# Squared-ReLU attention with two feed-forward layers: kept blocks read by 512-byte pieces, queries permuted, rounding on ScalarE

## The chip, the cores and the metric

The kernel runs on one core of one Trainium2 chip. The metric is the device time of one execution in microseconds (us), the median of several runs. TensorE (PE) does the matmuls, VectorE (DVE) and ScalarE (ACT) the elementwise work, SyncE (SP) issues nearly all DMAs. Each engine takes its instructions in the order of the program.

## The reference

Attention without softmax, then a feed-forward layer with a shrunk tanh, then a channel mix; all in float32.

```python
def _attn_ref(u, v, z):                      # u, v: (4, 3072, 256), z: (4, 3072, 64)
    scores = (1.0 / S) * np.matmul(z, z.transpose(0, 2, 1))
    attn = np.maximum(scores, 0.0) ** 2
    return u * np.matmul(attn, v)

def _moe_ref(x, w_in, w_out):                # w_in: (256, 2048)
    h = x @ w_in
    return (h - np.tanh(h)) @ w_out

def _moe2_ref(x, mu_k, mu_r, w_k, w_v, w_r): # w_k: (256, 1024)
    x_prev = np.concatenate([np.zeros((B, 1, D)), x[:, :-1, :]], axis=1)
    xk = mu_k * x + (1.0 - mu_k) * x_prev
    xr = mu_r * x + (1.0 - mu_r) * x_prev
    k = np.maximum(xk @ w_k, 0.0)
    r = 1.0 / (1.0 + np.exp(-(xr @ w_r)))
    return r * (k * k @ w_v)
```

`scores` is symmetric in queries and keys, so `attn` is too.

## The kernel before

**Precision.** Each float32 operand of a matmul is split into a high part, rounded to the matmul's own format, and a low part, the rest. A product takes three matmuls (`PASSES`: high with high, high with low, low with high). `copy_hi` (L83) rounds on ScalarE, `sub_lo` (L86) takes the rest on VectorE. For the scores the low and high parts of z lie in the two halves of the partitions, so two matmuls do: `z1` against `z1`, and `z1` against `z2`, which is `z1` with its halves swapped. `z_swap` (L123) makes it by two DMAs from `z1`.

**Tiles and units.** The 12288 rows are 24 tiles `t` of 512, six (`g` = 0 to 5) in each of four batches. A tile's attention is 12 units of 256 keys each (a pair of key chunks `kp`). A computed ("fresh") unit is 4 score matmuls, then on ScalarE Relu (L318) and Square (L319), on VectorE the rounding (L320, a CAST) and the low part (L87), and 12 matmuls with v into the tile's accumulator. Its names are `w_A` (PSUM), `a_A`, `h_A`, `l_A`. A unit's 12 matmuls come two units later (`LAG`).

**Kept blocks.** `attn` being symmetric, a block of 512 by 512 that tile i computed for keys j is what tile j needs for keys i, transposed. Tiles i = 0, 1 and 2 (`AGAIN` = 3) store such blocks to HBM (`keep`, L345), and tiles j > i read them again. `again_load` (L349) brings a block in by 16 DMAs of 64 KB in pieces of 128 bytes (32 elements), so that 32x32 transposes on VectorE finish the transposition. A re-read unit is: transpose (L373), rounding on ScalarE (L84), low part on VectorE (L87); its names are `b`, `t`, `h_t`, `l_t`. Tile g reads min(g, 3) blocks, two units each. In tiles g = 3, 4 and 5 re-read and fresh units alternate, which makes six pairs a tile (`pairs`, L327). From one pair to the next the order of tile 2 is fresh, fresh, re-read.

**The order.** The program is written out in one order (L666 to 681). At each unit n: the loads due at n go to SyncE's queue (`loads`), then the store of the unit before, then `produce` for unit n, `consume` for unit n - 2, `turned_high` for unit n + 1 (transpose and rounding, if it is a re-read unit), and `run_steps`. That takes side steps from a list sorted by due time until a budget of VectorE time is spent (L645), and takes what is overdue in any case. The side steps of the attention are: z (transpose, round, low part) and v (ScalarE copy, VectorE low part) for the next batch, u's transpose (`u_turn`), the product with u (`x1_steps`), and, up to the fourth batch, the conversion of the weights from 64-bit floats (`c_steps`, four steps of two to three VectorE instructions, names `cw_` and `c_`). In the fourth batch's last units the weights are split (`w_steps`).

**Buffers that matter.** `scratch` (four tiles: `a_A` and `t`), `hi` and `lo` (three each), two PSUM tiles for scores. A scratch tile that a store reads is free when the store has landed.

After the attention come the feed-forward layers, tile by tile, units H, K and R, with `x2_steps` (L480), `mix_steps` and `out_steps`.

## Time and profile before

| | |
|---|---|
| time, median of 3 runs | 2685.3 us (2685.24 to 2689.43) |
| profiled execution, its own time | 2691.05 us |
| its span, first to last instruction | 2689.3 us |
| PE busy | 2626.3 us (98%), 11424 matmuls |
| VectorE busy | 1738.7 us (65%) |
| ScalarE busy | 1271.8 us (47%) |
| DMA | 719738 packets, 663920 of them under 512 bytes |

The attention fills the first 1049 us, the feed-forward layers the rest. A matmul's record is about 0.39 us long, but matmuls are pipelined and the next one starts earlier, so the share of PE busy says little; the count of matmuls in a stretch against its length says how near PE is to its pace. An engine's idle time stands in brackets behind the instruction that ended it, with what released it. SPq is SyncE's sequencer, which issues the DMAs.

### The profile page before, as it was taken

To read this page: it belongs to the slowest core of one execution; us is meant where nothing else is said; L and a number is where in the kernel's file an instruction comes from. 1 tells how busy PE (TensorE), PEld (TensorE's weight loads), DVE (VectorE), ACT (ScalarE), POOL (GpSimd) and SP (SyncE) were. 2 spreads that over 40 slices of the span, in tenths; PEclk is the share of its full clock that TensorE was granted. 3 is DMA by queue.
4 is the path that set the end of the run, shared out by engine and by line. 5 is a ranking of instruction groups with operands and counts; after the bars stand their busy time and mean duration, and the time that the engine had idled before them with its cause. 6 is when DMAs were issued, how large, how long until landed. Compare 5 with 4: busy or idle time off the path is not lost.

```text
span 2689.3 us, 29169 instructions
## 1 busy us (share of the span) xinstructions
PE 2626.3 (98%) x11424; PEld 2149.4 (80%) x11424; DVE 1738.7 (65%) x1876; ACT 1271.8 (47%) x1386; POOL 0.2 (0%) x4
## 2 busy tenths in 40 slices
PE   8989998999999999999999999999999999999998
PEld 7767776777778887888888888888888888888887
DVE  8788878977996777555555555555555555555554
ACT  6444544454455545444444444444444444444443
POOL 0000000000000000000000000000000000000000
PEclk9999999999999999999999999999999999999999
DMA  8788568857876772000000000000000000000000
GB/s 199 185 171 174 149 174 171 175 166 181 160 160 192 175 126 104 8 16 16 16 17 16 16 16 16 16 16 16 16 16 16 16 16 16 16 16 17 16 8 16
DMA packets 719738, 204.07 MB, mean 76 GB/s; under 512 B 663920, under 2 KB 676208, under 8 KB 719600
## 3 DMA queue, kind: packets, MB, share of 16 engines
q1 hardware_dynamic: 718544, 202.08, 32.4%
q8 instruction: 89, 1.46, 0.2%
q14 instruction: 49, 0.40, 0.0%
q10 hardware_dynamic: 1056, 0.13, 0.0%
HBM read 114.03 MB, written 82.05 MB: 73 GB/s over the span
## 4 chain that ended last, share of the span: by engine, by line
PE 70%; SPq 15%; DVE 6%; DMA 4%; issue 3%; ACT 2%; DVEq 0%; ACTq 0%
PE acc_H L464 19%; PE w_H L408 19%; PE acc_K L464 10%; PE w_K L408 10%; SPq L355 9%; PE acc_A L464 7%; SPq L158 3%; PE w_R L432 2%; DMA b<-at 2%; SPq L99 1%; DVE t L373 1%; PE w_A L396 1%; PE w_A L395 1%; DVE h_A L320 1%; DVE l_A L87 1%
## 5 line engine op out<-in xcount | busy, mean ns | idle before, releaser
L464 PE MATMUL acc_A<-h_A,v 128*128 128x512 f32 x1536 | 504.7, 391 | 1.4 <-DVE h_A L320 1.4
L464 PE MATMUL acc_H<-h_H,w_out 128*128 128x512 f32 x1536 | 504.0, 389 | 0.0
L408 PE MATMUL w_H<-xh,w_in 128*128 128x512 f32 x1536 | 500.4, 389 | 0.0
L84 ACT ACTIVATE h_H<-g_H 128x1024 fp32r<-128x1024 f32 x192 | 203.7, 1061 | 386.1 <-DVE g_H L422 386.1
L87 DVE TENSOR_TENSOR l_H<-g_H,h_H 128x1024 fp32r<-128x1024 f32 x192 | 235.3, 1226 | 216.3 <-ACT h_H L84 216.3
L422 DVE TENSOR_TENSOR g_H<-w_H,g_H 128x1024 f32<-128x1024 f32 x192 | 233.6, 1217 | 171.2 <-ACT g_H L421 171.2
L464 PEld LDWEIGHTS acc_A<-h_A,v 128*128 128x128 f32 x1536 | 289.0, 188 | 63.3 <-DVE h_A L320 3.7
L464 PEld LDWEIGHTS acc_H<-h_H,w_out 128*128 128x128 f32 x1536 | 288.3, 188 | 59.8
L408 PEld LDWEIGHTS w_H<-xh,w_in 128*128 128x128 f32 x1536 | 288.3, 188 | 59.8
L421 ACT ACTIVATE g_H<-w_H 128x1024 f32<-128x1024 f32 x192 | 195.7, 1020 | 243.9 <-PE w_H L408 243.6
L464 PE MATMUL acc_A<-l_A,v 128*128 128x512 f32 x768 | 302.3, 394 | 8.7 <-DVE l_A L87 7.9
L408 PE MATMUL w_H<-x,w_in 128*128 128x512 f32 x768 | 298.8, 389 | 0.0
L464 PE MATMUL acc_H<-l_H,w_out 128*128 128x512 f32 x768 | 298.8, 389 | 0.0
L84 ACT ACTIVATE h_t<-t 128x1024 fp32r<-128x1024 f32 x96 | 101.9, 1062 | 353.6 <-DVE t L373 353.6
L318 ACT ACTIVATE a_A<-w_A 128x1024 f32<-128x1024 f32 (+1 forms) x193 | 195.9, 1015 | 153.1 <-PE w_A L396 113.6
L464 PE MATMUL acc_A<-h_t,v 128*128 128x512 f32 x768 | 259.7, 401 | 0.0
L408 PE MATMUL w_K<-mkh,w_k 128*128 128x512 f32 x768 | 251.8, 389 | 0.0
L464 PE MATMUL acc_K<-h_K,w_v 128*128 128x512 f32 x768 | 251.8, 389 | 0.0
L87 DVE TENSOR_TENSOR l_A<-a_A,h_A 128x1024 fp32r<-128x1024 f32 (+1 forms) x193 | 235.5, 1220 | 6.6
L320 DVE CAST h_A<-a_A 128x1024 fp32r<-128x1024 f32 (+1 forms) x193 | 132.7, 688 | 116.2 <-ACT a_A L319 114.9
L319 ACT ACTIVATE a_A<-a_A 128x1024 f32<-128x1024 f32 (+1 forms) x193 | 203.9, 1057 | 6.1
L320 DVE CAST h_K<-a_K 128x1024 fp32r<-128x1024 f32 x96 | 66.7, 694 | 212.7 <-ACT a_K L319 212.7
(121 smaller groups left out, 3462.7 us busy)
## 6 DMA issues: line engine op xcount, KB each, us to landing
at<-a_A SPq DMA_DIRECT2D x96, 512.0 KB, 4.2
b<-at SPq DMA_DIRECT2D x768, 64.0 KB, 2.4
vr<-in_v_dram SPq DMA_DIRECT2D x24, 512.0 KB, 4.6
uin<-in_u_dram SPq DMA_DIRECT2D x192, 64.0 KB, 2.8
x1d<-x SPq DMA_DIRECT2D x24, 512.0 KB, 3.1
x<-x1d SPq DMA_DIRECT2D x24, 512.0 KB, 3.8
out_dram<-ot SPq DMA_DIRECT2D x192, 64.0 KB, 1.9
zin<-in_z_dram SPq DMA_DIRECT2D x94, 64.0 KB, 2.7
```

The lines of the kernel that those rows point to most:

```text
L84: nc.scalar.activation(out=o, in_=i, func=ACTF.Copy)
L87: nc.vector.tensor_tensor(out=o, in0=i, in1=hi.bitcast(F32), op=ALU.subtract)
L158: nc.sync.dma_start(out=a[32 * q : 32 * q + 32, c], in_=src[q])
L318: nc.scalar.activation(out=a[:, x], in_=w[:, x], func=ACTF.Relu, scale=sc)
L319: nc.scalar.activation(out=a[:, x], in_=a[:, x], func=ACTF.Square)
L320: nc.vector.tensor_copy(h[:, x], a[:, x])
L355: nc.sync.dma_start(out=t[32 * q : 32 * q + 32, c], in_=src[q, c])
L408: nc.tensor.matmul(w[:, j], ws[wt, f // 4][a][:, c, (f % 4) * P : (f % 4 + 1) * P], x[m][:, c], start=n == 0, stop=n == 3 * DC - 1,)
L421: nc.scalar.activation(out=g, in_=w, func=ACTF.Tanh)
L422: nc.vector.tensor_tensor(out=g, in0=w, in1=g, op=ALU.subtract)
L432: nc.tensor.matmul(w[:, d], ws["r", 0][a][:, c, d * P : (d + 1) * P], x[m][:, c], start=n == 0, stop=n == 3 * DC - 1,)
L464: nc.tensor.matmul(o[:, c], w[a][:, c * P : (c + 1) * P], s[m][:, j], start=p == 0 and j == 0 and n == 0, stop=p == last and j == 1 and n ...
```

## The change

- `again_load` reads a block by 4 DMAs of 256 KB, in pieces of 512 bytes (a whole 128-column row piece). Partition j of group q then holds rows m x 32 + j, m = 0 to 15, with 128 columns each.
- The transpose of a re-read unit is now two instructions, one for each key chunk, that pick their 32 columns out of each 128.
- Tiles 0 to 2, which keep blocks, work on permuted queries: column (a, b, i) of 4 x 4 x 32 stands at (b, a, i). For that there is `zq`, a permuted copy of `z1` on ScalarE, which is the moving operand of the scores, `z2` is made of it, u is transposed in two instructions into that order, re-read units of tiles 1 and 2 are written in it, and `x2_steps` puts the order back.
- In tiles g > 1 a fresh unit is rounded on ScalarE (`high=copy_hi`) and no longer on VectorE.
- The budget of side steps in tiles g > 1 is 2.1 at a fresh unit and 0.1 at a unit that is re-read (before 1.4 and 0.2), and what is left over, up to 1.0, or overspent is carried to the next unit, in the feed-forward layers too.

```diff
--- before.py
+++ after.py
@@ -41,6 +41,8 @@
 
 
 
+
+
     nc = tc.nc
     B, S, D = u.shape
     DQ = z.shape[2]
@@ -80,6 +82,13 @@
     zero = head[:, 4 * DC : 4 * DC + 1]
     x1d = [dr.tile([P, DC, TB], F32, name=f"x1d{t}") for t in range(NT)]
 
+    def swapped(x):
+
+        return x.rearrange("p (a b i) -> p b a i", a=4, b=4)
+
+    def columns(x):
+        return x.rearrange("p (a b i) -> p a b i", a=4, b=4)
+
     def copy_hi(o, i):
         nc.scalar.activation(out=o, in_=i, func=ACTF.Copy)
 
@@ -87,7 +96,7 @@
         nc.vector.tensor_tensor(out=o, in0=i, in1=hi.bitcast(F32), op=ALU.subtract)
 
 
-    zin, z1, z2, vraw, vs, uin, uT = {}, {}, {}, {}, {}, {}, {}
+    zin, z1, zq, z2, vraw, vs, uin, uT = {}, {}, {}, {}, {}, {}, {}, {}
 
     def z_load(b, g):
 
@@ -112,19 +121,24 @@
         def low():
             t, w = st["t"], st["w"]
             sub_lo(w[DQ:], t[DQ:], w[DQ:])
+            if g < AGAIN:
+                q = p2(f"zq_{b}_{g}", F32R)
+                copy_hi(columns(q), swapped(w.bitcast(F32)))
+            else:
+                q = w
             if b == 0 and g == 0:
                 z2[0] = w2 = p2("z2_0", F32R)
-                sub_lo(w2[:DQ], t[:DQ], w[:DQ])
-                copy_hi(w2[DQ:], t[DQ:])
-            z1[b, g] = w
+                sub_lo(columns(w2[:DQ]), swapped(t[:DQ]), swapped(w[:DQ]))
+                copy_hi(columns(w2[DQ:]), swapped(t[DQ:]))
+            z1[b, g], zq[b, g] = w, q
 
         return [(1.7, lambda: (high(), low()))]
 
     def z_swap(t):
         b, g = divmod(t, NG)
         w = p2(f"z2_{t}", F32R)
-        nc.sync.dma_start(out=w[:DQ].bitcast(F32), in_=z1[b, g][DQ:].bitcast(F32))
-        nc.sync.dma_start(out=w[DQ:].bitcast(F32), in_=z1[b, g][:DQ].bitcast(F32))
+        nc.sync.dma_start(out=w[:DQ].bitcast(F32), in_=zq[b, g][DQ:].bitcast(F32))
+        nc.sync.dma_start(out=w[DQ:].bitcast(F32), in_=zq[b, g][:DQ].bitcast(F32))
         z2[t] = w
 
     def v_load(b, g):
@@ -164,9 +178,16 @@
     def u_turn(t):
         a = uin.pop(t)
         w = p4(f"uT{t}")
-        nc.vector.transpose(
-            out=w.rearrange("p c t -> p (c t)"), in_=a.rearrange("p c k i -> p (c k i)")
-        )
+        if t % NG < AGAIN:
+            for c in range(DC):
+                nc.vector.transpose(
+                    out=w[:, c].rearrange("p (b a i) -> p b a i", a=4, b=4),
+                    in_=a[:, c].rearrange("p (a b) i -> p b a i", a=4),
+                )
+        else:
+            nc.vector.transpose(
+                out=w.rearrange("p c t -> p (c t)"), in_=a.rearrange("p c k i -> p (c k i)")
+            )
         uT[t] = w
 
 
@@ -310,14 +331,14 @@
     def scratch(name):
         return sb.tile([P, 2, 512], F32, tag="e", name=name, bufs=4)
 
-    def square_split(name, w, sc, pieces=1):
+    def square_split(name, w, sc, pieces=1, high=nc.vector.tensor_copy):
         a = scratch(f"a_{name}")
         h, l = parts(name)
         for j in range(pieces):
             x = slice(2 * j // pieces, 2 * (j + 1) // pieces)
             nc.scalar.activation(out=a[:, x], in_=w[:, x], func=ACTF.Relu, scale=sc)
             nc.scalar.activation(out=a[:, x], in_=a[:, x], func=ACTF.Square)
-            nc.vector.tensor_copy(h[:, x], a[:, x])
+            high(h[:, x], a[:, x])
             sub_lo(l[:, x], a[:, x], h[:, x])
         return a, h, l
 
@@ -348,11 +369,10 @@
 
     def again_load(b, g, i):
 
-        t = sb.tile([P, 4, 16, 32], F32, tag="big", name=f"b{b}_{g}_{i}", bufs=12)
-        src = kept[b, i, g].rearrange("(k j) (c a i) -> a c j k i", j=32, c=4, i=32)
-        for c in range(4):
-            for q in range(4):
-                nc.sync.dma_start(out=t[32 * q : 32 * q + 32, c], in_=src[q, c])
+        t = sb.tile([P, 16, 4 * 32], F32, tag="big", name=f"b{b}_{g}_{i}", bufs=12)
+        src = kept[b, i, g].rearrange("(m j) (q x) -> q j m x", j=32, q=4)
+        for q in range(4):
+            nc.sync.dma_start(out=t[32 * q : 32 * q + 32], in_=src[q])
         blocks[b, g, i] = t
 
     def is_again(n):
@@ -367,12 +387,18 @@
         t, q = divmod(n, NP)
         b, g = divmod(t, NG)
         kp = pairs[g][q]
-        x = blocks[b, g, kp // 2][:, kp % 2 * 2 : kp % 2 * 2 + 2]
+        x = blocks[b, g, kp // 2]
         a = scratch(f"t_{t}_{q}")
         h, l = parts(f"t_{t}_{q}")
-        nc.vector.transpose(
-            out=a.rearrange("p c t -> p (c t)"), in_=x.rearrange("p c k i -> p (c k i)")
-        )
+        for j in range(2):
+            f = kp % 2 * 2 + j
+            y = x[:, :, f * 32 : f * 32 + 32]
+            if g < AGAIN:
+                y = y.rearrange("p (c k) i -> p k c i", c=4)
+                o = a[:, j].rearrange("p (k c i) -> p k c i", k=4, c=4)
+            else:
+                o = a[:, j].rearrange("p (m i) -> p m i", i=32)
+            nc.vector.transpose(out=o, in_=y)
         copy_hi(h, a)
         turned[n] = (a, h, l)
 
@@ -392,9 +418,12 @@
             for j in range(2):
                 kc = 2 * kp + j
                 lhsT = z1[b, kc // 4][:, (kc % 4) * P : (kc % 4 + 1) * P]
-                nc.tensor.matmul(w[:, j], lhsT, z1[b, g], start=True, stop=False)
+                nc.tensor.matmul(w[:, j], lhsT, zq[b, g], start=True, stop=False)
                 nc.tensor.matmul(w[:, j], lhsT, z2[t], start=False, stop=True)
-            a, *split[unit] = square_split(name, w, scale, 2 if t == 0 and p == 0 else 1)
+            a, *split[unit] = square_split(
+                name, w, scale, 2 if t == 0 and p == 0 else 1,
+                copy_hi if g > 1 else nc.vector.tensor_copy,
+            )
             if (b, g, kp // 2) in kept:
                 stores[n + 1] = lambda: keep(b, g, kp, a)
         elif kind in ("H", "K"):
@@ -483,7 +512,10 @@
             x2t[i] = []
             for c in range(DC):
                 x = p2(f"x2_{i}_{c}")
-                nc.scalar.activation(out=x, in_=o[:, c], func=ACTF.Copy)
+                if i % NG < AGAIN:
+                    nc.scalar.activation(out=columns(x), in_=swapped(o[:, c]), func=ACTF.Copy)
+                else:
+                    nc.scalar.activation(out=x, in_=o[:, c], func=ACTF.Copy)
                 x2t[i].append(x)
 
         return [(0.2, f)]
@@ -633,7 +665,7 @@
         n = at["K", i, NK - 1] + LAG
         task(n, n + 2, out_steps, i)
     tasks.sort(key=lambda x: x[:3])
-    ready = []
+    ready, spare = [], [0.0]
 
     def run_steps(n):
 
@@ -642,7 +674,10 @@
             ready.append((x[0], list(x[3](*x[4]))))
         ready.sort(key=lambda x: x[0])
         kind = units[min(n, len(units) - 1)][0]
-        left = {"A": 0.2 if is_again(n) else 1.4, "H": 2.2, "K": 2.4, "R": 4.0}[kind]
+        left = {"A": 1.4, "H": 2.2, "K": 2.4, "R": 4.0}[kind]
+        if kind == "A" and n // NP % NG > 1:
+            left = 0.1 if is_again(n) else 2.1
+        left += spare[0]
         while ready and (left > 0 or ready[0][0] <= n):
             for x in list(ready):
                 if left > 0 or x[0] <= n:
@@ -651,6 +686,7 @@
                     left -= cost
                     if not x[1]:
                         ready.remove(x)
+        spare[0] = min(left, 1.0)
 
     with tc.manual_schedule():
         z_load(0, 0)
```

What this makes of the order is shown at three places. The first is ScalarE in the second batch's tile 3 (unit 9) to tile 4 (unit 1). `h_t_` and `a_A_` carry the unit's number in the tile. ScalarE's order before:

```order
L318 ACTIVATE a_A_9_3700<-w_A_9_3695 128x1024
L319 ACTIVATE a_A_9_3700<-a_A_9_3700 128x1024
L84 ACTIVATE h_t_10_3720<-t_10_3719 128x1024
L318 ACTIVATE a_A_11_3747<-w_A_11_3742 128x1024
L319 ACTIVATE a_A_11_3747<-a_A_11_3747 128x1024
L84 ACTIVATE h_t_0_3767<-t_0_3766 128x1024
L318 ACTIVATE a_A_1_3824<-w_A_1_3819 128x1024
L319 ACTIVATE a_A_1_3824<-a_A_1_3824 128x1024
L84 ACTIVATE h_t_2_3844<-t_2_3843 128x1024
```

Three operations repeat there, a Relu, a Square and a round of t. ScalarE's order over the same units after the change:

```order
L339 ACTIVATE a_A_9_3508<-w_A_9_3503 128x1024
L340 ACTIVATE a_A_9_3508<-a_A_9_3508 128x1024
L93 ACTIVATE h_A_9_3509<-a_A_9_3508 128x1024
L93 ACTIVATE h_t_10_3528<-t_10_3527 128x1024
L93 ACTIVATE zq_0_3538<-z_2_0_3534 128x512
L339 ACTIVATE a_A_11_3558<-w_A_11_3553 128x1024
L340 ACTIVATE a_A_11_3558<-a_A_11_3558 128x1024
L93 ACTIVATE h_A_11_3559<-a_A_11_3558 128x1024
L93 ACTIVATE h_t_0_3578<-t_0_3577 128x1024
L93 ACTIVATE zq_1_3592<-z_2_1_3588 128x512
L339 ACTIVATE a_A_1_3628<-w_A_1_3623 128x1024
L340 ACTIVATE a_A_1_3628<-a_A_1_3628 128x1024
```

Behind each Square stands one more operation (`h_A`), and a `zq` stands between a round of t and the next Relu.

The second is VectorE over the same units, where `zt_` and `z_` are z's side step, `cw_` the weights' conversion. VectorE's order before:

```order
L373 STREAM_TRANSPOSE t_10_3719<-b_3_2_3429 128x1024
L109 STREAM_TRANSPOSE zt_1_3724<-zin_1_3601 128x512
L110 CAST z_2_1_3725<-zt_1_3724 128x512
L87 TENSOR_TENSOR z_2_1_3725<-zt_1_3724,z_2_1_3725 64x512
L87 TENSOR_TENSOR l_t_10_3721<-t_10_3719,h_t_10_3720 128x1024
L320 CAST h_A_11_3748<-a_A_11_3747 128x1024
L87 TENSOR_TENSOR l_A_11_3749<-a_A_11_3747,h_A_11_3748 128x1024
L373 STREAM_TRANSPOSE t_0_3766<-b_4_0_3549 128x1024
L204 TENSOR_SCALAR cw_in_1_3771<-c_in_1_3655 128x512
L208 SCALAR_TENSOR_TENSOR cw_in_1_3771<-c_in_1_3655,cw_in_1_3771 128x512
L211 TENSOR_SCALAR cw_in_1_3771<-c_in_1_3655 128x512
L87 TENSOR_TENSOR l_t_0_3768<-t_0_3766,h_t_0_3767 128x1024
```

Side steps stand there wherever a unit's budget lets them. VectorE's order over the same units after the change:

```order
L96 TENSOR_TENSOR l_t_10_3529<-t_10_3527,h_t_10_3528 128x1024
L96 TENSOR_TENSOR l_A_11_3560<-a_A_11_3558,h_A_11_3559 128x1024
L401 STREAM_TRANSPOSE t_0_3577<-b_4_0_3383 128x512 x2
L225 TENSOR_SCALAR cw_in_1_3583<-c_in_1_3475 128x512
L229 SCALAR_TENSOR_TENSOR cw_in_1_3583<-c_in_1_3475,cw_in_1_3583 128x512
L232 TENSOR_SCALAR cw_in_1_3583<-c_in_1_3475 128x512
L118 STREAM_TRANSPOSE zt_1_3587<-zin_1_3421 128x512
L119 CAST z_2_1_3588<-zt_1_3587 128x512
L96 TENSOR_TENSOR z_2_1_3588<-zt_1_3587,z_2_1_3588 64x512
L96 TENSOR_TENSOR l_t_0_3579<-t_0_3577,h_t_0_3578 128x1024
L96 TENSOR_TENSOR l_A_1_3630<-a_A_1_3628,h_A_1_3629 128x1024
```

The CAST (L320) is gone from between the transposes and the low part of A, the transposes are two, and side steps (`cw_`, `zt`, `z_`) stand only between a transpose and the low part of t.

The third is SyncE's queue around the swap for tile 2 of the first batch (`z_2`), with the kept blocks `b_2_0` and `b_2_1` and the stores (`at_`). SyncE's order before:

```order
L355 DMA b_2_0_760<-at_0_2_89 32x16x32 x16
L183 DMA c_in_1_777<-in_moe_w_in_dram 128x1024
L347 DMA at_1_5_98<-a_A_6_739 128x2x512
L347 DMA at_1_5_98<-a_A_7_785 128x2x512
L126 DMA z_2_823<-z_0_2_194 64x512
L127 DMA z_2_823<-z_0_2_194 64x512
L240 DMA wd_in_706<-cw_in_1_868 128x512
L158 DMA uin_928<-in_u_dram 32x16x32 x8
L355 DMA b_2_1_937<-at_1_2_90 32x16x32 x16
```

The swap (L126, L127) stands behind two stores and ahead of the next kept block. SyncE's order at the same place after the change:

```order
L375 DMA b_2_0_757<-at_0_2_89 32x16x128 x4
L204 DMA c_in_1_762<-in_moe_w_in_dram 128x1024
L368 DMA at_1_5_98<-a_A_6_735 128x2x512
L368 DMA at_1_5_98<-a_A_7_770 128x2x512
L140 DMA z_2_809<-zq_2_202 64x512
L141 DMA z_2_809<-zq_2_202 64x512
L261 DMA wd_in_702<-cw_in_1_855 128x512
L172 DMA uin_915<-in_u_dram 32x16x32 x8
L375 DMA b_2_1_924<-at_1_2_90 32x16x128 x4
```

The order of the queue is the same; each group of kept-block issues has 4 in place of 16, and the swap reads `zq`.

## Rows read from the trace of the kernel before

**Rows 1.** Windows, tiles 0–2 and 3–5 of each batch: length, engines' busy (count), clock

```profile
0.00:144.30 144.30, 132.37 (x557) 105.85 (x557) 113.18 (x139) 77.87 (x78) 0.20 (x4) 0.99 0.77 191
144.30:270.10 125.80, 115.02 (x478) 91.36 (x477) 110.79 (x134) 54.77 (x55) 0.00 (x0) 0.96 0.82 171
270.10:413.60 143.50, 136.83 (x582) 109.10 (x580) 112.22 (x138) 74.21 (x73) 0.00 (x0) 0.99 0.62 163
413.60:537.40 123.80, 113.80 (x477) 90.08 (x476) 110.52 (x134) 54.47 (x55) 0.00 (x0) 0.97 0.83 172
537.40:681.70 144.30, 137.23 (x582) 109.96 (x580) 112.53 (x138) 74.40 (x73) 0.00 (x0) 0.98 0.67 177
681.70:799.50 117.80, 111.90 (x478) 88.20 (x477) 110.19 (x134) 54.38 (x55) 0.00 (x0) 1.00 0.82 163
799.50:931.50 132.00, 131.77 (x582) 108.77 (x581) 92.66 (x92) 78.72 (x78) 0.00 (x0) 1.00 0.68 179
931.50:1049.10 117.60, 115.25 (x502) 94.91 (x501) 87.14 (x81) 58.00 (x59) 0.00 (x0) 0.99 0.60 128
```

**Rows 2.** Waits: engine and line, waited for what: us in total, times, longest

```profile
ACT a_A L318 <- DMA at<-a_A: 30.2, 11, 7.2
...
PE w_A L396 <- DMA z<-z: 7.4, 3, 3.5
```

**Rows 3.** SyncE's issues (duration ns min/median/max) and two landings from the chain

```profile
L355 SPq DMA_DIRECT2D b<-at x768: 302/487/3113, 57.7 to 1007.9; - x192
...
L347 SPq DMA_DIRECT2D at<-a_A x96: 359/434/1211, 16.6 to 926.4; - x96
...
66.25 3.25 DMA at<-a_A
...
90.10 5.69 DMA z<-z
```

**Rows 4.** Timeline of ScalarE and VectorE, fourth batch: start us, us, instruction

```profile
954.28 1.06 ACT L84 ACTIVATE h_t<-t 128x1024 fp32r<-128x1024 f32 x1 [3.49 <-DVE t L373]
955.24 1.01 ACT L318 ACTIVATE a_A<-w_A 128x1024 f32<-128x1024 f32 x1
955.37 1.23 DVE L87 TENSOR_TENSOR l_t<-t,h_t 128x1024 fp32r<-128x1024 f32 x1 [1.19 <-ACT h_t L84]
956.28 1.06 ACT L319 ACTIVATE a_A<-a_A 128x1024 f32<-128x1024 f32 x1
957.38 0.70 DVE L320 CAST h_A<-a_A 128x1024 fp32r<-128x1024 f32 x1 [0.78 <-ACT a_A L319]
958.11 1.23 DVE L87 TENSOR_TENSOR l_A<-a_A,h_A 128x1024 fp32r<-128x1024 f32 x1
959.25 1.24 DVE L373 STREAM_TRANSPOSE t<-b 128x1024 f32<-128x1024 f32 x1
960.58 1.06 ACT L84 ACTIVATE h_t<-t 128x1024 fp32r<-128x1024 f32 x1 [3.24 <-DVE t L373]
```

**Rows 5.** Timeline of the first batch's side steps on ScalarE and VectorE

```profile
219.96 0.38 DVE L204 TENSOR_SCALAR cw_in<-c_in 128x512 int32<-128x512 int32 x1
...
221.32 1.22 DVE L87 TENSOR_TENSOR l_t<-t,h_t 128x1024 fp32r<-128x1024 f32 x1
...
242.24 0.71 DVE L109 STREAM_TRANSPOSE zt<-zin 128x512 f32<-128x512 f32 x1
...
243.44 0.69 DVE L87 TENSOR_TENSOR z<-zt,z 64x512 fp32r<-64x512 f32 x1
...
247.37 1.06 ACT L84 ACTIVATE h_t<-t 128x1024 fp32r<-128x1024 f32 x1 [4.30 <-DVE t L373]
...
248.33 1.05 ACT L84 ACTIVATE v<-vr 128x1024 fp32r<-128x1024 f32 x1
```

**Rows 6.** Timeline at the program's start

```profile
11.53 1.01 ACT L318 ACTIVATE a_A<-w_A 128x1024 f32<-128x1024 f32 x1
...
13.93 0.69 DVE L87 TENSOR_TENSOR z<-zt,z 64x512 fp32r<-64x512 f32 x1
```

## The prediction, made before the changed kernel ran

> **What bounds the kernel now.** I read the windows by batch first [rows 1]. In the fourth batch's tiles 0 to 2 the matmuls run without a gap: 582 in 132.0 us, 0.2267 us each. Every stretch can be held against that pace, and what is over is TensorE time lost. Tiles 3 to 5 of the four batches lose 125.8 - 478 x 0.2267 = 17.4, 15.7, 9.4 and 3.8 us, 46.3 in all. Tiles 0 to 2 lose 18.0, 11.6, 12.4 and 0.1, together 42.1. The feed-forward part behind them is hardly touched by the diff, so only these 88 us are in play. They have two sources.
>
> The first is SyncE's queue. The waits show ScalarE held 30.2 us by stores of kept blocks that had not landed (their scratch tile is to be used again), and TensorE 7.4 us by the z swap [rows 2]. Behind both stands the same thing: 768 issues of 64 KB at about 0.49 us, 16 in a row for each kept block [rows 3]. Sixteen take 16 x 0.53 = 8.5 us with the step between them, and a store or a swap behind them starts that much later. The rows of the chain show one store landing after 3.25 us and one swap after 5.69 [rows 3].
>
> The second is a ring of two in-order engines. In tiles 3 to 5 re-read and computed units alternate. ScalarE does: round t, Relu, Square; VectorE does: round A (CAST), A's low part, transpose of the next t, and that releases ScalarE's next round. From one round of t to the next it is 954.28 to 960.58, 6.30 us [rows 4]. TensorE needs 28 matmuls per pair, 28 x 0.2267 = 6.35. So the ring stands 0.05 us under TensorE's pace, and any step put on it is lost. The fourth batch, which has no side work until its last units, shows that it just holds.
>
> **Part 1, the loads.** 16 issues per block become 4, 768 become 192. Price of one issue: the 512 KB store takes 0.434 us, the 64 KB load 0.487 [rows 3], so bytes don't set it; 4 x 0.53 = 2.1 us stand where 8.5 stood, and a store or swap behind is 6.4 us earlier. That covers the stall of most of these waits. Of the 42.1 us of tiles 0 to 2 I keep 10 for the program's start (TensorE's first matmul can't run until z is there) and 6 for VectorE's side steps, and book 26 as gone. The bounds are 7.4 (the swaps alone [rows 2]) and 32 (all but the start). That the fourth batch loses 0.1 us with the same loads says that the queue hurts only together with the c, z and v loads, and these stay. In tiles 3 to 5 the queue's share is dealt with below, since there I add up what the new program has instead.
>
> **Part 2, ScalarE rounds A.** The ring of the new order, piece by piece [rows 4]: round t to Relu 0.96; Relu to Square 1.04; Square to the new round 1.06 + 0.03, as Relu's 1.01 is followed by Square at 1.04; from that round to A's low part 1.09, as from 954.28 to 955.37; low part to transpose 1.14. The transpose is now two of 128x512, one of which takes 0.71 [rows 5]: 0.62 to the second, 0.71 and 0.09 to the release, 1.42 for 1.33 before. Sum 0.96 + 1.04 + 1.09 + 1.09 + 1.14 + 1.42 = 6.74 us. VectorE's CAST (0.70) leaves an engine that was waiting there anyway; on the ring 1.83 us becomes 2.18. The excess over TensorE is 0.39 us a pair, and 17 rounds a batch give 6.6 us. About 1 us of it is covered by the lead with which a batch enters tile 3 where side work doesn't eat it.
>
> Here a page bears on a term. Round t and the independent Relu behind it stand 0.96 apart for a length of 1.06, while Square, which reads what Relu wrote, starts 0.03 after its end [rows 4]. The Trainium skill (ScalarE: Activation LUTs, What ACT_TABLE_LOAD costs) says that back-to-back ACTIVATEs overlap by about 93 ns; by that alone the new round would come 0.97 after Square, the ring would be 6.62 and the forecast about 8 us lower. The new round reads Square's output, so I take the dependent pair.
>
> **Part 3, side steps.** They now stand between the transpose and the low part of t, and the budget carries what was overspent. VectorE has 1.19 us of idle time there and, with the CAST gone, the wait for ScalarE's third operation behind it, so steps of some 3 us fit. What was lost to steps between low part and CAST (idle 0.78 [rows 4], steps of 1.1 to 1.4) goes. I book 1.3 us a batch for the slots in which v's low part must wait for its copy. The v copies stay on ScalarE's ring: 247.37 to 248.33, 0.96 each [rows 5], 3 to 4 a batch, 2.9 to 3.8 us.
>
> **Part 4, the permuted queries.** For tiles 0 to 2 a copy zq is added on ScalarE, nine of them (three per later batch) in tiles 4 and 5 of the batch before, right behind a round of t and ahead of the next Relu. It reads z's low part, the last of three VectorE steps of the same slot. From the start of z's transpose to the end of that low part it is 242.24 to 244.13, 1.89 us [rows 5]. The transpose starts about 0.17 before ScalarE's round, so zq starts 1.76 after it, takes about 0.6 (between half of 1.06 and the whole), and Relu starts at 2.30 in place of 0.96: 1.34 on the ring. In two of three slots a c step stands ahead, 219.96 to 221.32, 1.36 us [rows 5]: 2.70 each. 1.34 + 2.70 + 2.70 = 6.7 us for each of the first three batches. The bounds are 0 (TensorE far enough ahead) and 8. The permuted reads and writes are priced as the plain ones; no row shows one, and the bounds for a transpose are 0.71 and twice that.
>
> At the program's start zq of the third z tile stands ahead of the second unit's Relu. That Relu runs at 11.53, and the z step ends at 13.93 + 0.69 [rows 6]; with 0.6 for zq it runs at 15.2, 3.7 later, and TensorE has no other work. The first matmul too now waits for a ScalarE copy, 0.6. With what follows I take 5 us (bounds 1 and 7).
>
> **The sum.** Tiles 3 to 5 after: 6.6 + 2.9 + 6.7 + 1.3 - 1.0 = 16.5 in the first batch, 17.4 in the second and third, 6.6 + 3.8 (the weights at the end, as now) = 10.4 in the fourth; 61.7 for 46.3, **+15.4**. Tiles 0 to 2: **-26 + 5**. In the feed-forward tail the second mixing copy now runs ahead of a K unit's squares: +0.5. Together -5 us. The profiled execution took 2691.05 us (span 2689.3), 5.7 over the median of the three runs, 2685.3; I carry the difference over: **2680 us**. About 0.2%, 5.4 us, is what a measurement of this kernel can tell from no change, so the forecast lies at that border.
>
> **Rivals.** *The ring doesn't bind.* If ScalarE's handoffs overlap as the independent ones do, or TensorE's lead covers the z copies, some 15 to 25 us of the 61.7 are not lost: 2655 to 2672. For it: VectorE is relieved, and its queue had the largest overruns. Against: the ring held only by 0.05 us, and every step added is longer. *Slower: the split transposes.* Two strided 128x512 transposes per re-read unit lie on the ring, 136 in the 68 rounds. At 0.71 us each the forecast stands; each 0.04 more costs 5 us and takes the gain away, and from about 0.79 it is 11 us worse, slower by over 0.2%; at 0.85 it would be 2699. The order bears it out; no row shows such a pattern. *The queue isn't relieved:* if a 256 KB load held the queue four times as long, the 26 us stay: 2706. The 512 KB store's 0.434 us speaks against. *The clock.* TensorE would wait a little in every pair. In the second stretch, with long waits, the granted clock was 0.96; in the third batch's tiles 3 to 5, 9.4 us lost in short waits, it was 1.00 [rows 1]. If it fell to the lower level (1.2 of 2.4 GHz) in 7 of the 68 pairs, each would take 6.35 more: +44, 2724. The Trainium skill (TensorE: Matmul & The Clock Gate, A second HAM failure mode) tells of a kernel whose frequent micro-idles did that; the 1.00 speaks against it here.
>
> **How the numbers follow.** The sum as it stands, 2673 to 2688: 0.50, of which a little under half lies below 2679.9. The ring that doesn't bind: 0.24. Slower transposes: 0.17. The queue not relieved 0.05, the clock 0.04. Faster by over 0.2%: 0.22 + 0.24 = 0.46; slower by over 0.2%: 0.15 + 0.05 + 0.04 = 0.24, the start of the slower transposes still within; the rest, 0.30, is no change. The range takes in the first three: 2657 to 2697.
>
> **What would show it.** In the fourth batch's tiles 3 to 5 the rounds of t should stand 6.74 us apart, and that stretch should lose about 10 us. ScalarE's waits for stores should fall from 30.2 to under 8 us and the swaps' 7.4 to about 1. Relu of the second unit should start near 15 us or later. Around each zq ScalarE should stand idle 0.7 to 2.2 us. A distance of 6.4 or less between rounds, or a loss of under 12 us in the second batch's tiles 3 to 5, would make the forecast wrong towards faster; transposes over 0.79 us towards slower.

## The result and the profile after

The changed kernel takes 2707.6 us, median of 4 runs (2707.25 to 2708.13), against 2687.0 for the kernel before on the same chip: a ratio of 1.0076, 95% interval 1.0059 to 1.0094. It is **slower by 20.6 us**, where 2680 was forecast with a range of 2657 to 2697. The profiled execution took 2708.1 us, its span is 2706.3.

The windows are cut as those of before were [rows 1]: each begins at the first matmul of a batch's tile 0, or at tile 3's first matmul with v, the last one at the second H unit. The columns are length, then PE, PEld, DVE, ACT and POOL busy with their counts, granted clock, DMA share, GB/s. The last row is the feed-forward part.

```profile
0.00:142.80 142.80, 131.60 (x556) 106.05 (x557) 108.06 (x141) 87.56 (x89) 0.20 (x4) 1.00 0.76 210
142.80:268.40 125.60, 113.89 (x477) 89.30 (x477) 95.77 (x125) 76.07 (x77) 0.00 (x0) 0.99 0.68 151
268.40:402.30 133.90, 132.63 (x581) 108.59 (x580) 111.16 (x147) 82.11 (x80) 0.00 (x0) 1.00 0.65 193
402.30:527.90 125.60, 113.93 (x478) 89.34 (x478) 95.77 (x125) 76.11 (x77) 0.00 (x0) 0.99 0.68 153
527.90:663.30 135.40, 132.99 (x581) 108.47 (x580) 110.92 (x147) 81.94 (x80) 0.00 (x0) 1.00 0.65 192
663.30:791.80 128.50, 115.20 (x478) 90.51 (x477) 95.87 (x125) 76.23 (x77) 0.00 (x0) 0.97 0.65 144
791.80:923.80 132.00, 131.78 (x582) 108.71 (x580) 90.53 (x101) 85.30 (x84) 0.00 (x0) 1.00 0.65 186
923.80:1049.10 125.30, 120.10 (x501) 93.68 (x500) 76.95 (x81) 78.19 (x78) 0.00 (x0) 0.99 0.45 113
1049.10:2690.00 1640.90, 1630.85 (x7165) 1343.03 (x7165) 884.94 (x887) 741.16 (x867) 0.00 (x0) 1.00 0.07 16
```

The same feed-forward stretch of the kernel before:

```profile
1049.10:2673.00 1623.90, 1623.90 (x7166) 1344.66 (x7165) 885.38 (x887) 743.92 (x867) 0.00 (x0) 1.00 0.07 16
```

By the pace of 0.2267 us a matmul, tiles 0 to 2 of the four batches now lose 142.8 - 556 x 0.2267 = 16.8, then 2.2, 3.7 and 0.1, together 22.7 for 42.1 before. Tiles 3 to 5 lose 17.5, 17.2, 20.1 and 11.7, together 66.6 for 46.3. In these two executions the two cancel: the last window begins at 1049.1 us in both kernels, and the difference of the spans, 17.0 us, lies behind it. But the profiled execution of before, 2691.05 us, lies 4.0 over the median of 2687.0; by the medians some 4 us of the 20.6 belong to the attention, as k1 below shows. The feed-forward matmuls, 7166 and 7165 of them, fill 1623.9 us before and 1640.9 after, **17.0 us more**, in a part that the prediction called hardly touched.

The waits name the place (engine and line, waited for what: us in total, times, longest):

```profile
ACT zq L93 <- DVE z L96: 22.2, 12, 3.0
...
PE w_H L437 <- DVE g_H L451: 10.1, 22, 0.5
ACT a_A L339 <- DMA at<-a_A: 8.3, 3, 5.3
```

`w_H <- g_H` is not among the waits of before; 22 times, once for each tile but the first and the last, TensorE waits 0.46 us for VectorE's `w - tanh`. The stores' row, 30.2 us before [rows 2], is down to 8.3, and the z swap's, 7.4, is gone.

### The profile page after: what moved, and what is told of

Its sections match the earlier page's. It is cut to its first block, busy times and chain, and to the rows that moved or that the text cites. A ratio compares the mean times of both kernels' runs of the same rounds, so it can differ in the third digit from the quotient of the medians.

```text
span 2706.3 us, 28503 instructions
## 1 busy us (share of the span) xinstructions
PE 2631.3 (97%) x11424; PEld 2144.3 (79%) x11424; DVE 1674.3 (62%) x1880; ACT 1385.7 (51%) x1502; POOL 0.2 (0%) x4
## 3 DMA queue, kind: packets, MB, share of 16 engines
q1 hardware_dynamic: 414416, 202.04, 29.3%
## 4 chain that ended last, share of the span: by engine, by line
PE 68%; ACT 12%; DVE 11%; issue 4%; DMA 3%; SPq 2%; ACTq 0%; DVEq 0%
PE acc_H L493 19%; PE w_H L437 15%; PE acc_A L493 11%; PE w_K L437 10%; PE acc_K L493 7%; DVE t L401 3%; PE w_R L461 2%; ACT a_A L340 2%; ACT h_A L93 2%; ACT a_A L339 2%; DVE l_A L96 2%; DMA b<-at 2%; PE w_A L422 2%; PE w_A L421 2%; ACT h_t L93 1%
## 5 line engine op out<-in xcount | busy, mean ns | idle before, releaser
L437 PE MATMUL w_H<-xh,w_in 128*128 128x512 f32 x1536 | 507.0, 391 | 10.1 <-DVE g_H L451 10.1
L341 DVE CAST h_K<-a_K 128x1024 fp32r<-128x1024 f32 x96 | 66.6, 694 | 229.3 <-ACT a_K L340 229.3
L493 PE MATMUL acc_A<-l_t,v 128*128 128x512 f32 x384 | 158.8, 414 | 41.9 <-DVE l_t L96 40.5
```

The source lines that it names most:

```text
L341: high(h[:, x], a[:, x])
L437: nc.tensor.matmul(w[:, j], ws[wt, f // 4][a][:, c, (f % 4) * P : (f % 4 + 1) * P], x[m][:, c], start=n == 0, stop=n == 3 * DC - 1,)
L493: nc.tensor.matmul(o[:, c], w[a][:, c * P : (c + 1) * P], s[m][:, j], start=p == 0 and j == 0 and n == 0, stop=p == last and j == 1 and n ...
```

## The tail: what the carried budget does behind each tile's last H

VectorE behind the last H unit of the second tile, kernel before (start us, us, engine, line, operation):

```profile
1162.35 0.75 DVE L504 SCALAR_TENSOR_TENSOR mxr<-x,head,mxr 128x512 f32<-128x512 f32 x1
1163.02 0.69 DVE L511 CAST mkh<-mxk 128x1024 fp32r<-128x1024 f32 x1
1163.62 1.22 DVE L422 TENSOR_TENSOR g_H<-w_H,g_H 128x1024 f32<-128x1024 f32 x1
...
1167.71 1.22 DVE L87 TENSOR_TENSOR mkl<-mxk,mkh 128x1024 fp32r<-128x1024 f32 x1
```

And after:

```profile
1162.44 0.75 DVE L536 SCALAR_TENSOR_TENSOR mxr<-x,head,mxr 128x512 f32<-128x512 f32 x1
1163.11 0.69 DVE L543 CAST mkh<-mxk 128x1024 fp32r<-128x1024 f32 x1
1163.71 0.69 DVE L543 CAST mrh<-mxr 128x1024 fp32r<-128x1024 f32 x1
1164.31 1.22 DVE L96 TENSOR_TENSOR mkl<-mxk,mkh 128x1024 fp32r<-128x1024 f32 x1
1165.45 1.22 DVE L451 TENSOR_TENSOR g_H<-w_H,g_H 128x1024 f32<-128x1024 f32 x1
```

These steps fall due in the R unit of the tile before, two units behind the last H, whose budget is 4.0. Before, four mixing steps and one CAST (`mkh`) stand ahead of `g_H`, the `w - tanh` of the next tile's first H unit, then the 4.0 are spent. After, 1.0 has been carried from the K unit before, which had no side steps to run, and the CAST of `mrh` and the low part `mkl` follow in the same unit: 0.60 + 1.14 = 1.74 us more on VectorE ahead of `g_H`, which starts at 1165.45 where it started at 1163.62. There are two PSUM tiles for this work, so TensorE can't start the H unit two further on until `g_H` has read its tile:

```profile
1165.87 0.39 PE L437 MATMUL w_H<-xh,w_in 128*128 128x512 f32 x1
1166.71 0.50 PE L437 MATMUL w_H<-xh,w_in 128*128 128x512 f32 x1 [0.45 <-DVE g_H L451]
1167.05 0.40 PE L437 MATMUL w_H<-x,w_in 128*128 128x512 f32 x1
```

The matmul due 0.23 after 1165.87 starts at 1166.71, 0.61 late, and the one behind it another 0.11. These 22 waits are 68.8 us apart, where a tile's 300 matmuls need 300 x 0.2267 = 68.0: 0.8 us a tile, some 17 in all. Of the 1.74 us about 1.1 were TensorE's lead at this point; the rest is loss.

Of the two steps the longer one gets in by accident. The steps up to the CAST of `mrh` are booked at 0.2 + 6 x 0.8 = 5.0, which is all that there is. In floating point 2.2e-16 is left over, and since `run_steps` asks only whether `left > 0`, it runs the low part too, booked at 1.3. The CAST alone would have put 0.60 us ahead of `g_H`, less than the lead of 1.1 (an estimate from these rows; no run tried it).

## Experiments

All times are medians, each ratio against runs of the kernel before on the same chip. "Lost" is TensorE's time over its pace, summed over the start times of all matmuls (each start less the one before, less 0.2266 us), by the tile whose unit the matmul works for; the first column of it is the time of the first matmul. For the kernel before this gives 36.2 and 49.9 where the windows gave 42.1 (with the first 6.0) and 46.3, since a matmul cut by a window's edge is counted on both sides and the edges before the tiles 3 lie 16 matmuls behind those tiles' first one. The row of before comes from the execution that lay 4.0 us over its median, so it holds some 4 us of loss that a usual run doesn't have.

| kernel | us | ratio, 95% interval | first | tiles 0-2 | tiles 3-5 | feed-forward |
|---|---|---|---|---|---|---|
| before | 2687.0 | | 6.0 | 36.2 | 49.9 | 0.8 |
| changed | 2707.6 | 1.0076 (1.0059 to 1.0094) | 6.6 | 17.4 | 68.1 | 17.8 |
| k1 carry in the attention only | 2691.1 | 1.0014 (1.0005 to 1.0024) | 6.6 | 17.2 | 68.2 | 0.8 |
| k2 before + carry in the feed-forward | 2704.8 | 1.0059 (1.0044 to 1.0074) | 6.2 | 34.9 | 47.2 | 17.8 |
| k3 k1, VectorE rounds A | 2668.8 | 0.9931 (0.9917 to 0.9946) | 6.7 | 15.8 | 46.8 | 0.8 |
| k4 k1, VectorE copies zq | 2672.9 | 0.9947 (0.9932 to 0.9962) | 6.3 | 14.0 | 53.5 | 0.8 |
| k5 before + loads and permuted queries | 2674.8 | 0.9950 (0.9935 to 0.9965) | 6.9 | 15.0 | 55.3 | 0.8 |
| k6 before + ScalarE rounds A | 2692.7 | 1.0019 (1.0009 to 1.0028) | 6.1 | 39.6 | 49.3 | 0.8 |
| k7 k3 and k4 together | 2654.4 | 0.9877 (0.9862 to 0.9892) | 6.4 | 13.0 | 35.2 | 0.8 |
| k8 k5, VectorE copies zq | 2661.4 | 0.9904 (0.9887 to 0.9920) | 6.4 | 12.0 | 44.1 | 0.8 |
| k9 k5, 16 issues a block | 2684.6 | 0.9987 (0.9977 to 0.9996) | 6.7 | 29.0 | 53.1 | 0.8 |
| k10 k7, nothing carried | 2687.0 | 0.9995 (0.9986 to 1.0004) | 6.4 | 14.2 | 67.4 | 0.8 |
| k12 before, 4 issues of 128-byte pieces | 2659.1 | 0.9889 (0.9873 to 0.9906) | 5.9 | 15.9 | 38.4 | 0.8 |
| k13 k12, new budgets, carry in the attention | 2651.4 | 0.9861 (0.9846 to 0.9876) | 5.9 | 16.7 | 28.6 | 0.8 |
| k14 k10, budget 0.0 at re-read units | 2660.9 | 0.9903 (0.9887 to 0.9918) | 6.4 | 13.3 | 42.9 | 0.8 |
| k15 k7, only debt carried | 2660.5 | 0.9903 (0.9885 to 0.9920) | 6.5 | 17.9 | 34.7 | 0.8 |
| k16 k13, only debt carried | 2660.1 | 0.9900 (0.9885 to 0.9915) | 6.1 | 27.6 | 27.6 | 0.8 |

### The tail (k1, k2)

k1, against the changed kernel; k2 puts a carry with the opposite condition into the kernel before.

```diff
-        spare[0] = min(left, 1.0)
+        spare[0] = min(left, 1.0) if kind == "A" else 0.0
```

> The changed kernel, but left-over budget is carried in the attention only; in the feed-forward layers each unit starts with its own budget again. Theory (the carried budget puts two more VectorE steps, CAST of mrh and low part of mk, ahead of w - tanh in the unit behind each tile's last H): the 0.74 us that TensorE loses at each of 23 tiles go, 2707.6 - 17 = 2690.5. Rival (the tail's loss comes from the permuted copy of x2 or from something carried over from the attention): 2707.

> The kernel before, with nothing changed but the budget's left-over, up to 1.0, carried from unit to unit in the feed-forward layers. Theory (carry alone makes the tail's loss): 2687 + 17 = 2704, attention as before. Rival (needs the permuted x2 or the other order): 2687.

k1 took 2691.1 and loses 0.8 us in the feed-forward part; k2 took 2704.8, 17.8 more than before, with the same 22 waits (engine and line, waited for what):

```profile
PE w_H L408 <- DVE g_H L422: 10.0, 22, 0.5
```

The carry alone makes the loss in the feed-forward part, with or without the rest of the change. The permuted copy of x2 has no part in it. And k1 is still 4.1 us slower than the kernel before (interval 1.0005 to 1.0024): the rest of the change, too, costs a little and gains nothing.

### The parts of the change one by one (k5, k6, k3)

k5 is the changed kernel without the last two points of the change: no `high=copy_hi`, and the budget line of before with no `spare`.

> The kernel before with the 512-byte loads, the two transposes and the permuted queries (zq, z2, u, x2), but VectorE rounds A everywhere and the budgets are the old ones, nothing carried. Theory (the loads relieve SyncE's queue, the ring stays near TensorE's pace at 6.30 + 0.09 = 6.39 us a pair, zq still stands on ScalarE): tiles 0 to 2 lose about 23 us in place of 42, tiles 3 to 5 about 45 in place of 46, since what zq costs (up to 20) takes up what the queue gives back there; some 2668. Rival (old side-step slots with zq behind them cost more than the queue gives back): 2685 or more.

k5 took 2674.8, between theory and rival. Tiles 0 to 2 lose 15.0, better than expected, tiles 3 to 5 55.3, worse by 10; k8 below shows zq as most of it.

k6, the kernel before with the rounding moved:

```diff
-            nc.vector.tensor_copy(h[:, x], a[:, x])
+            high(h[:, x], a[:, x])
...
+                copy_hi if g > 1 else nc.vector.tensor_copy,
```

> The kernel before, with one thing changed: in tiles 2 to 5 ScalarE rounds A in place of VectorE. Theory (the ring): a pair takes 6.30 + 0.35 = 6.65 us against TensorE's 6.35, 17 times in four batches, 20 us more, of which side steps that VectorE now has room for give back a part: 2695 to 2707; in the fourth batch's tiles 3 to 5, without side work, rounds of t stand 6.65 apart. Rival (VectorE was the bound in those tiles): 2675 to 2685, rounds 6.35 apart.

ScalarE's rounds of t in k6's fourth batch (timeline, start us and us):

```profile
959.75 1.06 ACT L84 ACTIVATE h_t<-t 128x1024 fp32r<-128x1024 f32 x1 [2.51 <-DVE t L373]
...
966.42 1.06 ACT L84 ACTIVATE h_t<-t 128x1024 fp32r<-128x1024 f32 x1 [2.51 <-DVE t L373]
```

They stand 6.67 us apart, as the ring says, and tiles 3 to 5 of that batch lose 10.8 in place of 4.3. But the whole is only 5.7 us slower, not 8 to 20: in the other three batches tiles 3 to 5 lose 38.5 in place of 45.6. A likely reason, which no run isolates: in the old order 99 side instructions stand behind a low part of t and so ahead of A's CAST, in 51 slots, and the ring no longer waits for that CAST. The theory's ring is right, its price in the old order was too high.

k3 undoes the rounding in the changed kernel, where side steps hardly stand in that slot any more:

```diff
             a, *split[unit] = square_split(
                 name, w, scale, 2 if t == 0 and p == 0 else 1,
-                copy_hi if g > 1 else nc.vector.tensor_copy,
             )
```

> The changed kernel with carry in the attention only (2691.1 measured), and VectorE rounds A again in all tiles; loads, permuted queries and new budgets stay. Theory (ScalarE's rounding lengthens the ring by 0.36 us a pair): rounds of t in the fourth batch's tiles 3 to 5 go from 6.72 to 6.36 apart, tiles 3 to 5 lose some 6 us less a batch, 68 to 44: 2667 to 2675. Rival (the new budgets need VectorE free of the CAST, 2.1 us of side steps then delay it): 2685 or more.

2668.8, in the expected range; the fourth batch's rounds of t are 6.36 apart (969.23 and 975.59). Tiles 3 to 5 give back 21.4 us. So the change splits into four steps, each one measured with the ones before it: loads and permuted queries 2687.0 to 2674.8 (**-12.2**), the new budgets with carry in the attention 2674.8 to 2668.8 (**-6.0**), ScalarE's rounding 2668.8 to 2691.1 (**+22.3**), carry in the feed-forward layers 2691.1 to 2707.6 (**+16.5**).

### zq (k4, k8, k7)

One line, in k1, k5 and k3:

```diff
-                copy_hi(columns(q), swapped(w.bitcast(F32)))
+                nc.vector.tensor_copy(columns(q), swapped(w.bitcast(F32)))
```

> The changed kernel with carry in the attention only (2691.1), and zq copied by VectorE right behind z's low part in place of ScalarE. Theory (zq's price is ScalarE's wait for z's low part, 1.3, 2.7 and 2.7 us a batch, and the start's): three batches give back 5 to 6.5 us each, the start 2 to 4: 2670 to 2675. Rival (TensorE's lead covers the waits, or VectorE's copy stands on the ring in its turn): 2686 to 2691.

> The kernel before with 512-byte loads and permuted queries alone (2674.8 measured), zq copied by VectorE. Theory (zq on ScalarE is what the loads pay): the zq waits of 18.2 us go, tiles 3 to 5 of the first three batches lose 3 to 5 us less each, the start 2 to 3: 2658 to 2663. Rival (VectorE's side steps are the price, whoever copies): 2670 to 2675.

> Both of the two others: VectorE rounds A and copies zq; 512-byte loads, new budgets, carry in the attention only. Theory (the two prices add): 2648 to 2657. Rival (VectorE, with both, becomes what the ring waits for in the slots with side steps): 2668 or more.

2672.9, 2661.4 and 2654.4, all three in the theory's ranges: 18.2, 13.4 and 14.4 us less than the same kernels with zq on ScalarE. The prices of the rounding and of zq add up nearly (22.3 + 18.2 = 40.5 expected of k7, 36.7 measured).

### What the loads relieve (k9, k12)

k9 cuts each 512-byte load into four by rows; k12 is the kernel before with four 128-byte loads joined into one:

```diff
-        src = kept[b, i, g].rearrange("(k j) (c a i) -> a c j k i", j=32, c=4, i=32)
-        for c in range(4):
-            for q in range(4):
-                nc.sync.dma_start(out=t[32 * q : 32 * q + 32, c], in_=src[q, c])
+        src = kept[b, i, g].rearrange("(k j) (c a i) -> a j c k i", j=32, c=4, i=32)
+        for q in range(4):
+            nc.sync.dma_start(out=t[32 * q : 32 * q + 32], in_=src[q])
```

> The kernel with 512-byte loads and permuted queries alone (2674.8 measured), but each kept block is brought in by 16 issues of 64 KB again (four rows of 512 bytes for each partition). Theory (SyncE's issues are what the loads relieve): the issues' 8.5 us a block are back, tiles 0 to 2 lose about 36 us again in place of 15 and tiles 3 to 5 more than 55: 2692 to 2705. Rival (the 128-byte pieces load the DMA engines): it stays at 2673 to 2677.

> The kernel before, with one thing changed: a kept block comes in by 4 issues of 256 KB, still in pieces of 128 bytes, so that transposes, queries and everything else stay as before. Theory (issues): tiles 0 to 2 lose some 17 in place of 36, tiles 3 to 5 some 35 in place of 50, as there is no zq: 2650 to 2660. Rival (pieces): 2685 to 2690, the four issues take as long as the sixteen did.

k9 took 2684.6, between theory and rival: 16 issues lose 29.0 us in tiles 0 to 2 where 4 lose 15.0, so the count of issues is worth most of it. Tiles 3 to 5 lose no more than with 4 (53.1 for 55.3), which the theory had wrong. The kernel before, 16 issues of 128-byte pieces, loses 36.2 in tiles 0 to 2; the piece may have a share in that, but the two kernels differ in zq and the transposes too. k12 took 2659.1, as the theory said: with 4 issues the 128-byte pieces lose 15.9, about as much as the 512-byte ones, and since nothing is permuted, no zq and no split transpose stand on the ring. SyncE's issues of the kept blocks (duration ns min/median/max) in the changed kernel, k9 and k12:

```profile
L375 SPq DMA_DIRECT2D b<-at x192: 303/487/2062, 57.6 to 997.7; - x192
```

```profile
L376 SPq DMA_DIRECT2D b<-at x768: 302/430/2100, 57.6 to 1004.4; - x192
```

```profile
L354 SPq DMA_DIRECT2D b<-at x192: 560/1384/5249, 54.2 to 969.9; - x192
```

An issue of 256 KB in 512-byte pieces takes 0.487 us like one of 64 KB in 128-byte pieces [rows 3], while 256 KB in 128-byte pieces take 1.384. The count of pieces in an issue orders these, not the bytes: 128 pieces (k9) 0.430, 512 in both sizes 0.487, 2048 (k12) 1.384. Four times the pieces take less than three times as long, so joining pays: a block's four issues in k12 take 5.3 us from the first's start to the last's end, the sixteen of before 8.9 (medians of 48 blocks), and k12's waits for stores and swaps are 12.3 and 1.7 us for 30.2 and 7.4 [rows 2]:

```profile
ACT a_A L318 <- DMA at<-a_A: 12.3, 5, 5.1
...
PE w_A L395 <- DMA z<-z: 1.7, 2, 1.1
```

### The budget and the carry in the attention (k13, k10, k14, k15, k16)

k13 is k12 with the new budgets and k1's carry. k10 is k7 without `spare`.

> The same 4 issues of 128-byte pieces, with the new budgets, and carry in the attention only. Theory (issues, and side steps between a transpose and its low part cost less): rounds of t 6.30 apart in the fourth batch, 2640 to 2650, below all others. Rival (pieces): 2680 or more.

> The kernel with VectorE rounding A and copying zq (2654.4 measured), without any carried budget in the attention either. Theory (the carry moves side steps by a unit here and there, the budgets of 2.1 and 0.1 do the work): 2651 to 2658. Rival (the carry is what spreads the steps): 2665 or more.

k13 is the fastest of all, 2651.4, 1.4 us over its expected range, 36 us below the kernel before and 56 below the changed one. k10 came out 29 us over the theory's range, as its rival said: without the carry tiles 3 to 5 lose 67.4 where k7 loses 35.2. VectorE in k10, behind a low part of t:

```profile
504.18 1.22 DVE L96 TENSOR_TENSOR l_t<-t,h_t 128x1024 fp32r<-128x1024 f32 x1
505.32 0.42 DVE L239 TENSOR_SCALAR c_out<-cw_out 128x512 int32<-128x512 int32 x1
...
506.72 0.69 DVE L341 CAST h_A<-a_A 128x1024 fp32r<-128x1024 f32 x1
```

A step of the weights stands between `l_t` and A's CAST, 1.40 us on the ring. The budget there is 0.1, and since 0.1 is over zero one whole step is run whenever one is ready, unless a debt from the unit before has been carried. In k10's order 88 side instructions stand in that slot, in k7's 25. k14, k15 and k16 ask whether the debt or the surplus counts:

```diff
-            left = 0.1 if is_again(n) else 2.1
+            left = 0.0 if is_again(n) else 2.1
```

```diff
-        spare[0] = min(left, 1.0) if kind == "A" else 0.0
+        spare[0] = min(left, 0.0)
```

> The kernel without any carry that measured 2687.0, with one number changed: the budget of a re-read unit is 0.0 in place of 0.1, so that no side step that isn't overdue is put behind a low part of t. Theory (the carry's worth in the attention is its debt: it keeps side steps out of the slot behind the low part of t; without it 88 side instructions stand there, with it 25, here 7): 2650 to 2660, as with carry (2654.4). Rival (the carry's worth is that left-over budget spreads the steps): 2675 or more.

> The kernel with VectorE rounding A and copying zq (2654.4 with carry in the attention only), with another carry: in all layers only what was overspent is carried, nothing left over. Theory (the surplus is what harms the feed-forward layers, the debt is what helps the attention): the feed-forward layers lose under 1 us as before the change, the whole 2650 to 2660. Rival (any carry harms there): 2664 or more.

> The kernel before with 4 issues of 128-byte pieces and the new budgets (2651.4 with carry in the attention only), only overspent budget carried, in all layers. Theory: as with the other carry, 2645 to 2655. Rival (left-over budget matters in the attention, or debt harms the feed-forward layers): 2660 or more.

k14, with 7 instructions in that slot and no carry at all, took 2660.9, a us over its range but 26 below k10: most of the debt's worth is that slot. Tiles 3 to 5 still lose 42.9 there for k7's 35.2, so the slot isn't all of it. k15 took 2660.5, half a us over its range; it loses 0.8 us in the feed-forward part, and in tiles 3 to 5 as little as k7: in the feed-forward layers debt does no harm, surplus does. The surplus is not without worth, though: without it tiles 0 to 2 lose more in both, 17.9 for 13.0 and 27.6 for 16.7, and k16 is 9 us behind k13, as its rival said. Why there stays open; in tiles 0 and 1 the budget is 1.4 at every unit.

## Why the prediction was wrong, step by step

**The tail, +0.5, was the term that failed: +17.0.** The prediction called the feed-forward part hardly touched by the diff, though the carry works in every unit of it. The order showed that the second mixing copy had moved up. I put it ahead of a K unit's squares and priced it at 0.5 in all, without setting the shift against TensorE's lead. That is its place at the last tile alone, where it costs nothing (`mrh` at 2663.66, ahead of a K unit's CAST at 2665.40; TensorE doesn't wait there). At 22 other tiles it stands ahead of an H unit's `w - tanh`, together with a low part. The trace of before had what was needed: the two steps' lengths, the place of `g_H`, the start of the matmul that needs its PSUM tile, and the count of tiles. The stretch lost nothing before, and I took that for room.

**Tiles 0 to 2, -26 + 5 = -21: -19.4 measured in the profiles.** The stores' waits fell to 8.3 (under 8 forecast), the swaps' vanished (about 1). The rival in which the queue isn't relieved falls. The price of an issue, one duration whatever the bytes, holds for the change (0.487), but partly by luck: bytes don't set it, pieces do, as k12 shows, and the new issue happens to have as many of them as the old one, 512. The Trainium skill (Perfetto Trace Analysis, What "DMA-bound" means) says that an issuing engine's solid DMA slices are descriptor generation, and that large descriptors are what matters. 0.487 against 1.384 us for the same 256 KB agrees; k12, as good with small pieces in few issues, shows that here the larger part was had without larger pieces.

**The ring, 6.74 us: 6.73 measured.** The fourth batch, ScalarE and then VectorE:

```profile
969.43 1.06 ACT L93 ACTIVATE h_t<-t 128x1024 fp32r<-128x1024 f32 x1 [2.56 <-DVE t L401]
970.40 1.01 ACT L339 ACTIVATE a_A<-w_A 128x1024 f32<-128x1024 f32 x1
971.44 1.06 ACT L340 ACTIVATE a_A<-a_A 128x1024 f32<-128x1024 f32 x1
972.53 1.06 ACT L93 ACTIVATE h_A<-a_A 128x1024 fp32r<-128x1024 f32 x1
976.16 1.06 ACT L93 ACTIVATE h_t<-t 128x1024 fp32r<-128x1024 f32 x1 [2.57 <-DVE t L401]
...
974.77 1.30 DVE L401 STREAM_TRANSPOSE t<-b 128x512 f32<-128x512 f32 x2
```

From 969.43 to 976.16; Square to the new round 1.09, as taken from the dependent pair [rows 4]. The rule of the Trainium skill that was weighed there (ScalarE: Activation LUTs, What ACT_TABLE_LOAD costs) would by the prediction's estimate have given 0.97 and 6.62. The trace agrees with it for the independent pair, round of t and Relu, 0.97 apart, and decides against it for the dependent one. The rival in which the ring doesn't bind falls (its 2655 to 2672, besides, answer to 8 to 25 us and not to the 15 to 25 that it names), and so does the one of slow split transposes: 192 of them take 0.665 to 0.707 us, the pair 1.30.

**zq, 1.34 and 2.70 us on the ring: 1.28 and 2.68 measured.** ScalarE at the program's start, and in tile 4 without and with a weights step ahead:

```profile
16.10 0.63 ACT L93 ACTIVATE zq<-z 128x512 fp32r<-128x512 f32 x1 [3.02 <-DVE z L96]
16.64 1.01 ACT L339 ACTIVATE a_A<-w_A 128x1024 f32<-128x1024 f32 x1
...
176.00 1.06 ACT L93 ACTIVATE h_t<-t 128x1024 fp32r<-128x1024 f32 x1 [2.56 <-DVE t L401]
177.72 0.63 ACT L93 ACTIVATE zq<-z 128x512 fp32r<-128x512 f32 x1 [0.66 <-DVE z L96]
178.25 1.01 ACT L339 ACTIVATE a_A<-w_A 128x1024 f32<-128x1024 f32 x1
...
184.01 1.06 ACT L93 ACTIVATE h_t<-t 128x1024 fp32r<-128x1024 f32 x1 [2.56 <-DVE t L401]
187.13 0.63 ACT L93 ACTIVATE zq<-z 128x512 fp32r<-128x512 f32 x1 [2.06 <-DVE z L96]
187.67 1.01 ACT L339 ACTIVATE a_A<-w_A 128x1024 f32<-128x1024 f32 x1
...
193.42 1.06 ACT L93 ACTIVATE h_t<-t 128x1024 fp32r<-128x1024 f32 x1 [2.56 <-DVE t L401]
```

From round of t to Relu it is 2.25 us without a weights step and 3.66 with one, in place of 0.97, and to the next round in the second case 9.41 in place of 6.73. At the start the second unit's Relu runs at 16.64 (near 15.2 or later forecast); k1's tiles 0 to 2 and first matmul against k4's give 3.5 us of the 5.

**Tiles 3 to 5, +15.4: +20.3 in the profiles.** The intervals of the ring and of zq came out to 0.06 us, but what they cost did not, and that the sum came near is partly luck. Of the forecast 61.7 us, 26.4 were the ring, 20.1 zq and 15.2 all the rest. Taken out one by one, the rounding gives back 21.4 (k3) and zq 14.7 (k4, where VectorE's copy costs something in turn), and k13, with neither zq nor ScalarE's rounding, still loses 28.6. So the rest, side steps above all, was booked at about half, and the two others too high. One slot shows it. The third batch has a slot in which six instructions of weights steps and v's low part stand between a transpose and the low part of t:

```profile
675.22 0.39 DVE L225 TENSOR_SCALAR cw_v<-c_v 128x512 int32<-128x512 int32 x1
...
677.42 1.23 DVE L96 TENSOR_TENSOR v<-vr,v 128x1024 fp32r<-128x1024 f32 x1 [0.76 <-ACT v L93]
678.57 0.42 DVE L239 TENSOR_SCALAR c_v<-cw_v 128x512 int32<-128x512 int32 x1
...
679.97 1.22 DVE L96 TENSOR_TENSOR l_t<-t,h_t 128x1024 fp32r<-128x1024 f32 x1
```

That is 4.75 us where I wrote that steps of some 3 us fit, and TensorE waits 3.5. The lead of 1.0 us with which a batch was to enter tile 3 can't be told apart from the other terms.

**The clock** stayed: 1.00 in the feed-forward stretch with its 22 waits, 0.97 or more in every other, so that rival falls.

So the sum missed the tail by 16 us and the attention by 10: -5.6 was forecast for it, and k1, the change without the tail's loss, is 4.1 over the kernel before (in the profiles the miss is 6.5, for the reason given above). Without the tail the time would have been in the range, but still slower and not faster. Each rival was a way for the attention to go otherwise; none asked what the same lines do in the other three fifths of the time. (The pace was read a little off: 132.0 us over 582 is 0.2268 and not 0.2267, which moves a stretch by 0.06 us at most.)

## What to carry to other kernels

A change to a rule (a budget, a carry, a priority) works wherever the rule is asked, so each place where it can move a step has to be priced, first of all the long stretches that lose nothing now: 1.7 us in a slot with a lead of 1.1, 22 times, made 16.5 of the 20.6 us here. A budget of decimal costs that is asked only whether it is over zero can be decided by a rounding remainder. On a ring of two engines that stands within 1% of the bound, moving work to the less busy engine lengthens the ring if the handoff gets longer (0.70 us off VectorE, 0.37 more a pair). And before a layout is permuted to make transfers larger, try to join the issues: the four-issue load of k12 got most of the queue's gain without any of the permutation's cost.

## What the runs showed of the hardware

Larger pieces took little from the DMA engines: the queue's packets fell from 718544 to 414416, but the time of all packets only from 32.4 to 29.3% of 16 engines' span (queue, packets, MB, share; before, then after).

```profile
q1 hardware_dynamic: 718544, 202.08, 32.4%
```

```profile
q1 hardware_dynamic: 414416, 202.04, 29.3%
```

A permuting read (pieces of 32 elements) costs ScalarE and VectorE nothing that can be seen: zq takes 0.63 us on ScalarE, as the first unit's Square of 128x512 at 11.29 does, and 0.43 on VectorE in k7, as the plain CAST of that size at 7.73 does there.
